# Attention, expert layer and soft mixture on one core: small steps and weight conversion spread over the rounds, reciprocals spread by DRAM transfers, chunk sums added on VectorE

## The chip, the core and the metric

The kernel runs on one core of one Trainium2 chip. The metric is the device time of one execution in microseconds (us), as the median of three runs. Engines are named as the profile names them: PE is TensorE (PEld its weight load), DVE is VectorE, ACT is ScalarE, POOL is GpSimd, and SP is SyncE, whose queue issues most of the transfers.

## The reference

```python
# attention: q, k, v are (4 batches, 12 heads, 448, 64)
q_n, k_n = rmsnorm(q, g_q), rmsnorm(k, g_k)
scores = q_n @ k_n.T / sqrt(64)
attn = exp(scores - max(scores)); attn = attn / (sum(attn) + 1e-9)
x = (attn @ v) as (1792, 768)
# expert layer: w_in (768, 2048), w_out (2048, 768)
y = relu(x @ w_in) ** 2 @ w_out
# soft mixture: phi (768, 32), w1 (8, 768, 1024), w2 (8, 1024, 768)
logits = y @ phi
d = softmax(logits, over tokens); slots = d.T @ y          # 32 rows
out_slots[e] = relu(slots[e] @ w1[e]) @ w2[e]
out = softmax(logits, over slots) @ out_slots
```

w_in and w_out arrive in 64-bit elements, so they are read as two 32-bit words each and turned into float32 by integer operations on the chip.

## The kernel before

Two heads of a batch make a pair; there are 24 pairs, six to a batch. A function `attention()` runs rounds t, and in each round the steps of a list, `ORDER` (lines 25 to 28). The table `blocks` gives every step an offset: in round t the loads are those of pair t+5, sums of squares and the root (a Newton iteration for 1/sqrt, on odd pairs and for two pairs at once) those of pair t+4, transposes t+3, row maxima t+2, scores (`s0` to `s3`), products with v (`v0` to `v3`) and the sums of exponentials t, and the reciprocals and the normalised output t-1. A pair's 448 rows are four chunks of 112; `nm` is a chunk's row maximum, `p_0` to `p_3` are its exponentials (112 x 896, both heads), `pss` the scores in PSUM.

The sums come from 16 instructions on PE with a matrix of ones (for each chunk four groups of rows). They are copied to `sm`, folded by small transfers into `rsh` (32 x 28), inverted there by VectorE (`rr`), sent back as two rows (`rs`), and spread over 128 partitions by PE with the 2 x 128 matrix `sel2`. VectorE multiplies the pair's output with that (`xf`), and splits it in two parts of reduced precision (`xh`).

Beside the attention the two weight matrices are converted in 32 units of 768 x 128, sixteen of each. A unit is fetched, gets three operations on VectorE (`wf`), two on ScalarE for the sign, one more on ScalarE, a product on POOL, and is stored to DRAM. A unit of w_out is also transposed on PE, copied (`wt`), and multiplied with phi (`wp`). The step `cvt` of a round calls `convert_stage`, which moves units on by a large stage: all three VectorE steps are issued at once. `CONVERT` says how many units may begin in each round.

Rounds before `PINNED` (6) keep their instructions in the order in which the program issues them (`InOrder`); in the later ones the tile scheduler may reorder. After the sixth pair of a batch a generator `moe_hidden(b)` begins, the hidden layer `ph` of that batch (16 columns of 18 products on PE, with the weights split as `whl` from the stored units); each step of `ORDER` gives it a credit of its cost times `PACE`. When the attention's buffers are released, the last batch's hidden layer and the experts follow, whose 1-MB weight pieces stream through a ring of buffers.

All helpers record through one line, so the profile names line 97 for nearly everything, and groups are told apart by their tiles.

Of the kernel before, what the change touches and what calls it, by code (L numbers as in the profile page):

```python
# [17 lines left out]
def raw(ap):  # L18
# [17 lines left out]
PINNED = 6  # L36
# [8 lines left out]
def tile_attention_moe_softmoe(  # L45
# [80 lines left out]
    sel2 = const.tile([2, 2, 64], F32, tag="sel2", name="sel2")  # L126
    nc.vector.tensor_copy(sel2, ident[0:2, 0:2, None].broadcast_to([2, 2, 64]))

# [94 lines left out]
    def root(t):  # L223
        if t % 2 == 0:
            return
        ss = live["ss"]
        ms = att.tile([CP, 32], F32, tag="ms", name=f"ms_{t}", bufs=2)
        y = att.tile([CP, 32], F32, tag="y", name=f"y_{t}", bufs=2)
        u = att.tile([CP, 32], F32, tag="u", name=f"u_{t}", bufs=2)
        dve.tensor_scalar(ms, ss, 1.0 / D, EPS, ALU.mult, ALU.add)  # L230
        dve.tensor_scalar(y.bitcast(I32), ms.bitcast(I32), 1, None, ALU.logical_shift_right)
        dve.tensor_scalar(y.bitcast(I32), y.bitcast(I32), -1, 0x5F3759DF, ALU.mult, ALU.add)
        for _ in range(3):
            dve.scalar_tensor_tensor(u, y, -0.5, y, ALU.mult, ALU.mult)
            dve.tensor_tensor(u, u, ms, ALU.mult)
            dve.scalar_tensor_tensor(y, u, 1.5, y, ALU.add, ALU.mult)
        for x in range(2):
            for i in range(2):
                a = 16 * x + 8 * i
                qk = live[t - 1 + x]["qk"][i]  # L240
                by = y[:, a : a + 8].rearrange("p (c h) -> p c h", h=2)[:, :, :, None]
                pool.tensor_tensor(qk, qk, by.broadcast_to([CP, NC, 2, D]), ALU.mult)
# [55 lines left out]
    def values(t, c):  # L298
# [3 lines left out]
        for j in range(2):  # L302
            for d in range(0, D, 32):
# [7 lines left out]
                )  # L311

    def sums(t):
        ps = mps()
        for x in range(2):
# [166 lines left out]
    def convert_next():  # L482
        convert_stage(True)
# [475 lines left out]
```

## Time and profile before

| what | us |
|---|---|
| median of 3 runs (lowest, highest) | 984.38 (982.26, 984.74) |
| profiled execution, device time | 984.84 |
| profiled execution, span from first to last instruction | 983.0 |
| PE busy | 832.9 (85%) |
| VectorE busy | 461.5 (47%) |
| ScalarE busy | 384.8 (39%) |
| POOL busy | 301.2 (31%) |

The mean granted clock of TensorE is 0.921 of full speed. A busy time is the sum of an engine's own instructions, so an engine at 85% may still be the limit in one stage and idle in another; the stages therefore stand apart in the rows below. The marks of the stages are events of the trace: 35.3 is the first instruction of PE, 68.5 the first scores of pair 0, 231.4 the end of the sums of pair 6, 440 that of pair 11, 760 that of pair 23.

### The profile page before, as it was taken

What the parts mean: (1) busy time and instruction counts of PE and PEld (TensorE: products, weight loads), DVE (VectorE), ACT (ScalarE), POOL (GpSimd) and SP (SyncE); (2) the same over time, 40 slices, a digit from 0 to 9 for tenths busy, and PEclk for the clock granted to TensorE, in tenths of its full rate; (3) what the DMA queues carried; (4) which work ended last, traced back from release to release, by engine and by line L of the source; (5) the groups of instructions that cost most, each with busy time, mean ns of one, the idle gap of its engine ahead of it and who ended that gap; (6) DMA issues with size and microseconds to landing.
All of it is one profiled execution on the core that took longest, in us unless ns stands there. A gap on an engine that the chain in (4) does not pass through costs nothing.

```text
span 983.0 us, 13480 instructions
## 1 busy us (share of the span) xinstructions
PE 832.9 (85%) x5298; PEld 490.5 (50%) x5298; DVE 461.5 (47%) x799; ACT 384.8 (39%) x598; POOL 301.2 (31%) x282
## 2 busy tenths in 40 slices
PE   0257777799888979989999998999999999889875
PEld 0133333345555646635566563556655588444433
DVE  4676575687832766455345346522312443411022
ACT  2435454566534555434334433433335243110011
POOL 4532323275734565320624323133222000000000
PEclk9999798759879989999999999999999899998795
DMA  8743333363253543202222220021121695699999
GB/s 270 211 123 95 121 110 110 102 194 98 97 157 95 180 154 112 77 26 65 63 62 64 78 77 26 28 74 42 49 59 34 236 367 184 253 370 363 347 348 294
DMA packets 113134, 142.87 MB, mean 145 GB/s; under 512 B 53296, under 2 KB 94768, under 8 KB 113072
## 3 DMA queue, kind: packets, MB, share of 16 engines
q1 hardware_dynamic: 100880, 84.61, 27.5%
q0 software_dynamic: 12192, 57.42, 18.1%
q8 instruction: 41, 0.67, 0.3%
q14 instruction: 21, 0.17, 0.1%
HBM read 123.57 MB, written 18.09 MB: 144 GB/s over the span
## 4 chain that ended last, share of the span: by engine, by line
PE 55%; DVE 12%; issue 8%; DMA 8%; POOL 7%; ACT 5%; SPq 4%; POOLq 0%; DVEq 0%; ACTq 0%
PE ph L97 18%; PE pm L97 16%; PE pss L97 6%; PE pv L97 6%; SPq L97 4%; PE pe L97 4%; DVE wf L97 4%; PE so_ps L97 2%; POOL whl L97 2%; PE pt L97 2%; DMA qk<-in_q_dram 2%; POOL wf L97 2%; DVE nm L97 2%; DMA wr<-wi_s 1%; DMA w<-in_moe_w_dram 1%
## 5 line engine op out<-in xcount | busy, mean ns | idle before, releaser
L97 PE MATMUL ph<-xh,whl 128*128 128x448 f32 x1152 | 281.0, 387 | 7.9 <-ACT gt L97 7.0
L97 PEld LDWEIGHTS ph<-xh,whl 128*128 128x128 f32 x1152 | 213.0, 194 | 68.7 <-issue 36.4
L97 DVE TENSOR_REDUCE nm<-pss 112x2 f32<-112x896 f32 x96 | 103.5, 1080 | 65.8 <-PE pss L97 65.6
L97 ACT ACTIVATE p<-pss 112x896 f32<-112x896 f32 x96 | 87.7, 915 | 89.3 <-PE pss L97 89.3
L97 POOL TENSOR_TENSOR whl<-wr,whl 128x768 fp32r<-128x768 f32 x45 | 84.5, 1877 | 123.3 <-ACT whl L97 116.6
L97 POOL TENSOR_TENSOR wf<-wf,w 128x768 f32<-128x768 f32 x32 | 64.5, 2018 | 141.9 <-ACT wf L97 116.5
L97 PE MATMUL pv<-p,vf 112*32 112x448 f32 x768 | 106.7, 595 | 0.3 <-ACT p L97 0.3
L97 ACT ACTIVATE gt<-ph 128x448 f32<-128x448 f32 x64 | 34.7, 542 | 122.8 <-PE ph L97 122.8
L97 ACT ACTIVATE w<-w 128x768 int32<-128x768 f32 (+2 forms) x68 | 58.6, 865 | 54.2 <-DVE wf L97 28.8
L97 POOL TENSOR_TENSOR gt<-gt 128x448 f32<-128x448 f32 x33 | 31.3, 949 | 152.6 <-ACT gt L97 146.0
L97 PE MATMUL pm<-ident,qk 112*128 112x112 f32 x192 | 31.7, 295 | 40.9 <-DMA vf<-in_v_dram 35.3
L97 PE MATMUL pss<-kh,qh 64*112 64x448 f32 x192 | 44.1, 453 | 25.8 <-DVE nm L97 16.8
L97 POOL TENSOR_TENSOR qk<-qk,y 112x512 f32<-112x512 f32 x48 | 49.5, 1054 | 32.9 <-DVE y L97 32.9
L97 PEld LDWEIGHTS pm<-ident,qk 112*128 112x128 f32 x192 | 22.9, 157 | 62.0 <-POOL qk L97 41.5
L97 PE MATMUL pm<-p,ones 112*32 112x448 f32 x384 | 50.5, 609 | 0.0
L97 DVE TENSOR_TENSOR ql<-pm,qh 128x448 fp32r<-128x448 f32 x24 | 15.0, 624 | 74.7 <-ACT qh L97 74.7
L97 PE MATMUL pss<-qh,kh 64*112 64x448 f32 x192 | 45.7, 468 | 4.3 <-ACT p L97 4.3
L97 DVE TENSOR_REDUCE ss<-sq 112x8 f32<-112x512 f32 x48 | 32.4, 676 | 30.5 <-ACT sq L97 30.3
L97 ACT CAST whl<-wr 128x768 fp32r<-128x768 f32 x50 | 41.3, 827 | 8.0 <-DMA wr<-wi_s 7.9
L97 ACT ACTIVATE sq<-qk 112x512 f32<-112x512 f32 x48 | 29.9, 625 | 32.5 <-DMA qk<-in_q_dram 26.4
L97 PEld LDWEIGHTS pss<-kh,qh 64*112 64x112 f32 x192 | 18.5, 187 | 46.9 <-DVE nm L97 25.8
L97 PE MATMUL pm<-ident,gt 128*112 128x128 f32 x256 | 39.1, 285 | 2.0 <-DVE lsb L97 1.6
(149 smaller groups left out, 1173.4 us busy)
## 6 DMA issues: line engine op xcount, KB each, us to landing
w<-in_moe_w_dram SPq DMA_DIRECT2D x48, 1024.0 KB
wr<-wi_s POOLq DMA_DIRECT2D x50, 384.0 KB, 3.4
w<-in_moe_w_in_dram POOLq DMA_DIRECT2D x16, 768.0 KB, 6.8
w<-in_moe_w_out_dram POOLq DMA_DIRECT2D x16, 768.0 KB, 5.7
wi_s<-wf POOLq DMA_DIRECT2D x16, 384.0 KB, 3.2
wo_s<-wf POOLq DMA_DIRECT2D x16, 384.0 KB, 2.9
wo<-wo_s SPq DMA_DIRECT2D x6, 1024.0 KB
qk<-in_q_dram SPq DMA_DIRECT2D x48, 112.0 KB
```

Of the source, the lines that this page charges most:

```text
L97: ins = f(*args, **kw)
```

## The change

There are five edits. The list `ORDER` is rewritten: loads, squares and roots run one pair further ahead, the transposes stand ahead of the last product with v, the output of a pair comes one round later and early in it, and seven rounds are held in written order. The root is cut in three steps. The conversion becomes a generator that does one small stage at each of four `cvt` slots of a held round, and three at a slot afterwards. The reciprocals go to a DRAM tile and are read back over 64 partitions each by two transfers (`rb`), and the product with `sel2` is gone. From pair 7 on VectorE adds exponentials of two chunks (`fold`), and PE sums half as many tiles.

```diff
 ORDER = (
-    "loadv load s0 mx0 cvt row sq0 s1 mx1 v0 cvt sq1 root recip "
-    "s2 mx2 v1 cvt s3 mx3 v2 out v3 sum trans0 trans1 cvt"
+    "loadv load s0 mx0 row sq0 cvt out s1 mx1 v0 sq1 cvt s2 mx2 v1 recip cvt root0 "
+    "s3 mx3 v2 cvt root1 trans0 trans1 v3 sum root2"
 ).split()
-LEAD = 5
-CONVERT = [1, 1, 1, 1, 1, 1, 2, 1, 2, 1, 2, 3, 3, 3, 3, 3, 3]
+LEAD = 6
+CONVERT = [1, 1, 1, 1, 1, 1, 1, 1, 1, 1, 1, 1, 1, 3, 3, 3, 3, 3, 3, 3]
-PINNED = 6
+PINNED = 7
...
+    def newton():
+        ms, y, u = live["root"]
+        dve.scalar_tensor_tensor(u, y, -0.5, y, ALU.mult, ALU.mult)
+        dve.tensor_tensor(u, u, ms, ALU.mult)
+        dve.scalar_tensor_tensor(y, u, 1.5, y, ALU.add, ALU.mult)
-    def root(t):
+    def root(t, part):
         if t % 2 == 0:
             return
...
+        if part == 0:
...
+        elif part == 1:
+            newton()
+            newton()
+        else:
+            newton()
+            for x in range(2):
...
+                    pool.tensor_tensor(qk, qk, by.broadcast_to([CP, NC, 2, D]), ALU.mult)
...
+        if c % 2 and t >= PINNED:
+            fold(t, c)
+    def fold(t, c):
+        p, p1 = live[t][f"p{c - 1}"], live[t][f"p{c}"]
+        dve.tensor_tensor(p1, p1, p, ALU.add)
     def sums(t):
         ps = mps()
-        for x in range(2):
+        folded = t >= PINNED
+        for x in (1,) if folded else (0, 1):
             for j in range(2):
                 for i in range(2):
                     g = 32 * (2 * j + i)
-                    mm(ps[g : g + 32, :S], ones, live[t][f"p{2 * x + i}"][:, j, :], x == 0, x == 1)
-        tt = att.tile([128, S], F32, tag="t", name=f"t_{t}", bufs=2)
+                    c = 2 * i + 1 if folded else 2 * x + i
+                    mm(ps[g : g + 32, :S], ones, live[t][f"p{c}"][:, j, :], folded or x == 0, x == 1)
+        tt = att.tile([128, S], F32, tag="t", name=f"t_{t}", bufs=3)
...
-        rs = att.tile([2, S], F32, tag="rs", name=f"rs_{t}", bufs=2)
+        rs = dram.tile([2, S], F32, tag="rs", name=f"rs_{t}", bufs=2)
         sp.dma_start(rs.rearrange("j (r e) -> j r e", r=16), rr)
-        live[t]["rs"] = rs
+        rb = att.tile([128, S], F32, tag="rb", name=f"rb_{t}", bufs=1)
+        for j in range(2):
+            sp.dma_start(rb[64 * j : 64 * j + 64, :], rs[j : j + 1, :].broadcast_to([64, S]))
+        live[t]["rb"] = rb
     def normalise(t):
-        tt, rs = live[t]["t"], live[t]["rs"]
-        ps = mps()
-        mm(ps[:, :S], sel2.rearrange("p j d -> p (j d)"), rs)
         x = xp.tile([128, S], F32, tag="xf", name=f"xf_{t}", bufs=6)
-        dve.tensor_tensor(x, tt, ps[:, :S], ALU.mult)
+        dve.tensor_tensor(x, live[t]["t"], live[t]["rb"], ALU.mult)
...
     blocks = {
-        "load": (5, 0, lambda t: load(t)),
+        "load": (6, 0, lambda t: load(t)),
-        "sq0": (4, 0, lambda t: square(t, 0)),
+        "sq0": (5, 0, lambda t: square(t, 0)),
...
-        "out": (-1, 0.8, lambda t: normalise(t)),
+        "out": (-2, 0, lambda t: normalise(t)),
     }
...
-        for t in range(-LEAD, NT + 1):
+        for t in range(-LEAD, NT + 2):
...
-                    convert_stage(todo > 0)
+                    convert_step(todo > 0, 1 if pin["on"] else 3)
...
         dve.tensor_scalar(fi, hi, 3, 0x40000000, ALU.logical_shift_left, ALU.bitwise_xor)
+        yield
         dve.scalar_tensor_tensor(fi, lo, 29, fi, ALU.logical_shift_right, ALU.bitwise_or)
+        yield
         dve.tensor_scalar(f, f, -3.0e38, 3.0e38, ALU.max, ALU.min)
...
         act.activation(lo, hi.bitcast(F32), AF.Copy, scale=0.500001 / SMALL)
+        yield
         act.activation(lo.bitcast(F32), lo, AF.Sign)
+        yield
         act.activation(f, f, AF.Abs)
         pool.tensor_tensor(f, f, lo.bitcast(F32), ALU.mult)
...
+    def convert_step(more, stages):
+        for unit in list(running):
+            for _ in range(stages):
+                if next(unit[2], 0) == 0:
+                    running.remove(unit)
+                    break
```

The first place is VectorE's queue in a held round with a root. Before, a conversion's three steps (`wf`) and the root (`ms`, `y`, `u`) stand together:

```order
L97 TENSOR_REDUCE nm_587<-pss_618 112x2
L97 TENSOR_SCALAR wf_631<-w_26_343 128x768
L97 SCALAR_TENSOR_TENSOR wf_631<-w_26_343,wf_631 128x768
L97 TENSOR_SCALAR wf_631<-wf_631 128x768
L97 TENSOR_REDUCE ss_443<-sq_1_637 112x8
L97 TENSOR_SCALAR ms_640<-ss_443 112x32
L97 TENSOR_SCALAR y_641<-ms_640 112x32
L97 TENSOR_SCALAR y_641<-y_641 112x32
L97 SCALAR_TENSOR_TENSOR u_642<-y_641 112x32
L97 TENSOR_TENSOR u_642<-u_642,ms_640 112x32
```

Now, in a round of that kind, row maxima (`nm`) stand between the steps of the conversion and between the parts of the root:

```order
L97 SCALAR_TENSOR_TENSOR wf_461<-w_11_247,wf_461 128x768
L97 TENSOR_REDUCE nm_445<-pss_500 112x2
L97 COPY wt_509<-pm_516 128x256
L97 TENSOR_SCALAR wf_461<-wf_461 128x768
L97 TENSOR_SCALAR ms_522<-ss_382 112x32
L97 TENSOR_SCALAR y_523<-ms_522 112x32
L97 TENSOR_SCALAR y_523<-y_523 112x32
L97 TENSOR_REDUCE nm_445<-pss_539 112x2
L97 COPY wp<-pm_547 128x32
L97 SCALAR_TENSOR_TENSOR u_524<-y_523 112x32
```

What moved is the row maximum: it no longer stands behind the whole root. The second place is PE's queue in a later round, with the hidden layer (`ph`) between the products of a pair. Before, the product with `sel` and eight rows for the sums (two instructions each) stand there:

```order
L97 MATMUL pv_1839<-p_2_1897,vf_1486 32x448 x4
L97 MATMUL pm_1985<-rs_1886,sel_85 128x448
L97 MATMUL ph_1994<-xh_1636,whl_1906 128x448 x9
L97 MATMUL pv_1839<-p_3_1963,vf_1486 32x448 x4
L97 MATMUL ph_1994<-xh_1636,whl_1906 128x448 x9
L97 MATMUL pm_2017<-p_0_1776,ones 32x448
L97 MATMUL pm_2017<-p_1_1815,ones 32x448
L97 MATMUL pm_2017<-p_0_1776,ones 32x448
L97 MATMUL pm_2017<-p_1_1815,ones 32x448
L97 MATMUL pm_2017<-p_2_1897,ones 32x448
L97 MATMUL pm_2017<-p_3_1963,ones 32x448
```

Now:

```order
L97 MATMUL pv_1743<-p_3_1853,vf_1456 32x448
L97 MATMUL pm_1890<-ident,qk_0_1117 128x112 x4
L97 MATMUL pm_1897<-ident,qk_1_1120 128x112 x4
L97 MATMUL pv_1743<-p_3_1853,vf_1456 32x448 x3
L97 MATMUL ph_1917<-xh_1680,whl_1820 128x448 x9
L97 MATMUL pm_1927<-p_1_1734,ones 32x448
L97 MATMUL ph_1917<-xh_1680,whl_1820 128x448
L97 MATMUL pm_1927<-p_3_1853,ones 32x448
L97 MATMUL pm_1927<-p_1_1734,ones 32x448
L97 MATMUL pm_1927<-p_3_1853,ones 32x448
```

The product with `sel` is gone, the sums read `p_1` and `p_3` alone, and the transposes of a later pair have come ahead of the last product with v. The third place is VectorE's queue between the reciprocals (`rr`) and the output (`xf`) that waits for them. Before, in a held round:

```order
L97 SCALAR_TENSOR_TENSOR rr_659<-rsh_549 32x28
L97 RECIPROCAL rr_659<-rr_659 32x28
L97 TENSOR_REDUCE nm_587<-pss_675 112x2
L97 TENSOR_REDUCE nm_587<-pss_699 112x2
L97 TENSOR_TENSOR xf_709<-t_545,pm_707 128x448
```

Now, where the two are nearest to each other, in a later round:

```order
L97 RECIPROCAL rr_3693<-rr_3693 32x28
L97 SCALAR_TENSOR_TENSOR y_3955<-u_3956,y_3955 112x32
L97 SCALAR_TENSOR_TENSOR u_3956<-y_3955 112x32
L97 TENSOR_TENSOR u_3956<-u_3956,ms_3954 112x32
L97 SCALAR_TENSOR_TENSOR y_3955<-u_3956,y_3955 112x32
L97 SCALAR_TENSOR_TENSOR u_3956<-y_3955 112x32
L97 TENSOR_TENSOR u_3956<-u_3956,ms_3954 112x32
L97 SCALAR_TENSOR_TENSOR y_3955<-u_3956,y_3955 112x32
L97 TENSOR_REDUCE nm_3565<-pss_3631 112x2
L97 TENSOR_TENSOR xf_3855<-t_3530,rb_3698 128x448
```

Here `xf` reads `rb`, which two transfers fill from DRAM, where it read a tile of PSUM that PE filled; seven small operations of a root and one row maximum stand between.

## Rows read from the trace of the kernel before

**Rows 1.** Busy time by stage: start:end, length, engines' busy time (instructions), clock, DMA share, GB/s
```profile
0.00:35.30 35.30, 0.00 (x0) 0.00 (x0) 16.30 (x43) 11.61 (x15) 16.17 (x25) 1.00 0.97 273
...
68.50:231.40 162.90, 129.97 (x810) 61.40 (x810) 112.40 (x192) 87.26 (x125) 61.66 (x56) 0.81 0.40 120
231.40:440.00 208.60, 183.16 (x1078) 114.88 (x1078) 119.40 (x180) 100.73 (x152) 104.15 (x95) 0.91 0.38 114
440.00:760.00 320.00, 310.73 (x1960) 183.26 (x1956) 128.35 (x229) 128.61 (x201) 99.52 (x90) 1.00 0.20 55
760.00:983.00 223.00, 193.59 (x1401) 121.01 (x1397) 62.18 (x120) 45.22 (x90) 2.74 (x2) 0.87 0.88 304
```

**Rows 2.** The same view by round, rounds 0 to 6 (order: PE, PEld, DVE, ACT, POOL)
```profile
68.50:87.70 19.20, 16.06 (x116) 8.53 (x115) 9.24 (x15) 9.79 (x14) 5.34 (x6) 0.91 0.39 124
87.70:114.90 27.20, 20.12 (x123) 9.12 (x122) 18.75 (x34) 13.44 (x19) 10.34 (x10) 0.81 0.38 118
114.90:133.00 18.10, 15.06 (x122) 7.88 (x121) 10.72 (x18) 9.63 (x14) 2.98 (x3) 1.00 0.33 99
133.00:160.60 27.60, 19.88 (x122) 8.67 (x121) 18.54 (x34) 13.39 (x19) 10.33 (x10) 0.81 0.38 114
160.60:180.25 19.65, 16.34 (x103) 6.64 (x103) 10.28 (x16) 9.16 (x13) 2.99 (x3) 0.83 0.32 94
180.25:209.70 29.45, 21.79 (x115) 10.44 (x114) 26.48 (x52) 17.87 (x26) 17.59 (x14) 0.66 0.45 126
209.70:231.40 21.70, 20.71 (x120) 10.11 (x120) 18.39 (x27) 13.98 (x22) 12.08 (x11) 0.75 0.55 162
```

**Rows 3.** Timeline of PE in round 1
```profile
100.48 0.46 PE L97 MATMUL pss<-kh,qh 64*112 64x448 f32 x2 [3.77 <-ACT p L97]
...
103.29 1.85 PE L97 MATMUL pm<-rs,sel 2*128 2x448 f32 x2 [0.73 <-DMA rs<-rr]
```

**Rows 4.** Chain of waits at 754 to 767: the sel product, the sums, the reciprocals' transfer
```profile
754.27 0.94 PE pm L97 x2
...
758.50 1.69 PE pm L97 x16
...
765.04 1.84 DMA rs<-rr
```

**Rows 5.** Timeline of VectorE in round 1
```profile
94.48 2.54 DVE L97 SCALAR_TENSOR_TENSOR wf<-w,wf 128x768 int32<-128x768 int32 x1
...
98.25 0.18 DVE L97 TENSOR_SCALAR ms<-ss 112x32 f32<-112x32 f32 x1
...
101.34 2.01 DVE L97 TENSOR_REDUCE nm<-pss 112x2 f32<-112x896 f32 x2
```

**Rows 6.** Timeline of PE before the first scores: start, length, instructions [idle before <-releaser]
```profile
47.45 1.54 PE L97 MATMUL pm<-ident,wf 128*128 128x128 f32 x6 [6.78 <-POOL wf L97]
...
66.54 2.01 PE L97 MATMUL pm<-ident,qk 112*128 112x112 f32 x8 [5.05 <-POOL qk L97]
```

**Rows 7.** DMA issues: count, KB each, us from issue to landing
```profile
wr<-wi_s POOLq DMA_DIRECT2D x50, 384.0 KB, 3.4
...
wo_s<-wf POOLq DMA_DIRECT2D x16, 384.0 KB, 2.9
```

**Rows 8.** VectorE's groups by form for three tiles: duration ns min/median/max, first and last start
```profile
L97 DVE TENSOR_TENSOR xf<-t,pm x24: 610/621/623, 105.2 to 768.0; 128x448 f32<-128x448 f32 x24
L97 DVE TENSOR_TENSOR xh<-xf,xh x24: 609/625/2081, 106.4 to 769.5; 128x448 fp32r<-128x448 f32 x24
...
L97 DVE TENSOR_TENSOR whl<-wi,whl x14: 948/952/960, 777.5 to 832.9; 128x768 fp32r<-128x768 f32 x14
```

**Rows 9.** PE's groups for a w_out unit: count | busy us, mean ns | idle before
```profile
L97 PE MATMUL pm<-phi_sb,wt 128*128 128x32 f32 x192 | 30.1, 304 | 8.2 <-ACT wt L97 5.9 <-DVE wt L97 2.2
...
L97 PE MATMUL pm<-ident,wf 128*128 128x128 f32 x96 | 17.2, 310 | 18.0 <-POOL wf L97 13.2 <-ACT sm L97 2.4 <-DVE kl L97 1.4
```

More of the change, by code (lines that the diff above doesn't have):

```diff
@@ L221, in square @@
         dve.tensor_reduce(live["ss"][:, a : a + 8], sq, AX.X, ALU.add)
-    def root(t):
+    def newton():
[4 more added lines that the diff above has]
+    def root(t, part):
         if t % 2 == 0:
             return
[L226 to L236, printed above, removed]
-        for x in range(2):
[L238 to L242, printed above, removed]
+        if part == 0:
+            ms, y, u = (att.tile([CP, 32], F32, tag=n, name=f"{n}_{t}", bufs=2) for n in ("ms", "y", "u"))
+            live["root"] = ms, y, u
+            dve.tensor_scalar(ms, live["ss"], 1.0 / D, EPS, ALU.mult, ALU.add)
+            dve.tensor_scalar(y.bitcast(I32), ms.bitcast(I32), 1, None, ALU.logical_shift_right)
+            dve.tensor_scalar(y.bitcast(I32), y.bitcast(I32), -1, 0x5F3759DF, ALU.mult, ALU.add)
+        elif part == 1:
[4 more added lines that the diff above has]
+            for x in range(2):
+                for i in range(2):
+                    a = 16 * x + 8 * i
+                    qk = live[t - 1 + x]["qk"][i]
+                    by = live["root"][1][:, a : a + 8].rearrange("p (c h) -> p c h", h=2)[:, :, :, None]
+                    pool.tensor_tensor(qk, qk, by.broadcast_to([CP, NC, 2, D]), ALU.mult)
     def trans(t, i):
@@ L350, in tile_attention_moe_softmoe @@
     blocks = {
[L351 removed]
+        "load": (6, 0, lambda t: load(t)),
         "loadv": (1, 0, lambda t: load_v(t)),
[L353 to L355 removed]
+        "sq0": (5, 0, lambda t: square(t, 0)),
+        "sq1": (5, 0, lambda t: square(t, 1)),
+        "root0": (5, 0, lambda t: root(t, 0)),
+        "root1": (5, 0, lambda t: root(t, 1)),
+        "root2": (5, 0, lambda t: root(t, 2)),
         "trans0": (3, 0.4, lambda t: trans(t, 0)),
@@ L419, in convert @@
         dve.tensor_scalar(fi, hi, 3, 0x40000000, ALU.logical_shift_left, ALU.bitwise_xor)
+        yield
         dve.scalar_tensor_tensor(fi, lo, 29, fi, ALU.logical_shift_right, ALU.bitwise_or)
+        yield
         dve.tensor_scalar(f, f, -3.0e38, 3.0e38, ALU.max, ALU.min)
[L422 to L425 removed]
         act.activation(lo, hi.bitcast(F32), AF.Copy, scale=0.500001 / SMALL)
+        yield
         act.activation(lo.bitcast(F32), lo, AF.Sign)
+        yield
         act.activation(f, f, AF.Abs)
         pool.tensor_tensor(f, f, lo.bitcast(F32), ALU.mult)
[L431 to L442 removed]
+        prefetch()
+        yield
+        yield
+        dst = wi_s if kind == "in" else wo_s
+        pool.dma_start(dst[fc], f.rearrange("p k f -> p (k f)"))
+        if kind == "out":
+            wt = wst.tile([128, KC, 128], F32, tag="wt", name=name("wt"), bufs=1)
+            pss = []
+            for a, z in ((0, 4), (4, KC)):
+                ps = mps()
+                for kc in range(a, z):
+                    pe.transpose(ps[:, (kc - a) * 128 : (kc - a + 1) * 128], f[:, kc, :], ident)
+                src = ps[:, : (z - a) * 128].rearrange("p (k f) -> p k f", f=128)
+                copy(ON_WT[1 + (a > 0)], wt[:, a:z, :], src)
+            yield
+            ps = mps()
+            for kc in range(KC):
+                mm(ps[:, :NS], wt[:, kc, :], phi_sb[:, kc, :], kc == 0, kc == KC - 1)
+            copy(ON_WT[0], wp[:, fc, :], ps[:, :NS])
     units = []
@@ L475, in convert_stage @@
                 fetched[key] = fetch64(*key)
-            w64 = fetched.pop(key)
-            signed.append((*key, w64, convert(*key, w64)))
-            prefetch()
-        if not (units or signed or stored):
+            gen = convert(*key, fetched.pop(key))
+            next(gen)
+            running.append((*key, gen))
+            if not state["h0"]:
+                prefetch()
+        if not (units or running):
             state["cv"] = False
     def convert_next():
-        convert_stage(True)
+        convert_step(True, 3)
     def ensure(kind, fc):
-        while any(u[:2] == (kind, fc) for u in units + signed + stored):
+        while any(u[:2] == (kind, fc) for u in units + running):
             convert_next()
```

36 lines of the change are left out of this document (2 added, 34 removed).

## The prediction, made before the changed kernel had run

> **What bounds the kernel now.** I read the busy times by stage first [rows 1], because the average over 983 us mixes stages with different limits. The reader is to see five of them. From the first score to the end of the seventh pair's sums (68.5 to 231.4) TensorE works 130 of 162.9 us at a granted clock of 0.81, and no other engine is above 113: nobody is full, so order and waits decide. From 231.4 to 440 it works 183 of 208.6, and from 440 to 760 it works 310.7 of 320: there every instruction taken from TensorE is time, and 9.3 us of idling is all that waits cost. From 760 on the DMA share is 0.88; that stage has no edit of this change but the end of the last pair. Before 68.5 TensorE has little to do and waits for operands.
>
> Then the stage that waits, round by round [rows 2]. A round with no root and one conversion lasts 18.1 to 19.65 us. A round with a root and two conversions lasts 27.2, 27.6 and 29.45. The difference, 8 to 10 us, comes every second round. TensorE's timeline in the first of the long rounds says where [rows 3]: 3.77 us for a tile of exponentials, then 0.73 for the reciprocals, and then a product at 1.85 for two instructions, twice the 0.94 that it costs late in the kernel [rows 4]. The granted clock of that round is 0.81, so part of it ran at the lower of the two levels, 1.2 instead of 2.4 GHz; it is 1.00 in the shortest round, which has no such gap. VectorE's timeline of the same place [rows 5] names the owner: from 94.48 a conversion step of 2.54 with the next step and a sum behind it, from 98.25 twelve small root operations and the reciprocal's two, and only at 101.34 two row maxima that the next scores want. Ahead of the stage TensorE waits in the same way twice, 6.78 for a converted tile that it is to transpose and 5.05 for the scaled q and k that the root feeds [rows 6].
>
> **The change part by part.**
>
> *Spread root and conversion, pinned rounds.* Work is not removed: the same three conversion steps and twelve root operations are issued, but at most one conversion step or six root operations stand between two row maxima. Seven rounds are now held in written order; by the end of the seventh thirteen units have been started instead of seventeen, so each round has one. A round then looks like the short rounds of before, plus half a root (fourteen operations from 98.25 to 101.34 are 0.22 each with their gaps, so twelve are 2.6 and half is 1.3 us). Of the short rounds I take the mean, 18.98 [rows 2], and leave the half root out because row maxima now stand between its parts and TensorE no longer waits for all of it at once. Bounds: 15.8 (what TensorE works in the short rounds, on average, so no wait left) and the present mean, 162.9/7 = 23.3. Sum: 7 x 18.98 = 132.9 in place of 162.9, so -30.0 (-52 to 0).
>
> *Start of the stage.* Loads run six pairs ahead and roots are a round earlier, so the 5.05 wait for scaled q and k should go, and the transposes of a converted tile stand at the round's end and no longer hold the queue for 6.78. But the loads share a DMA system that is at 0.97 until 35.3 [rows 1], and one more round of small work has to go through VectorE and POOL. Bounds: -11.8 (both waits gone) and +5.05 (the wait doubled, if the extra round of small work comes in series). I take -4, near the 5.05 of a root that is a round ahead; the other wait is for a unit's whole conversion, which nothing shortens.
>
> *Reciprocals by DRAM.* TensorE loses 24 products of two instructions, 0.94 each where the clock is 1.00 [rows 1, 4]; 17 of them lie between 231.4 and 760: 17 x 0.94 = 16.0, all of it in stages where TensorE is the limit. VectorE's xf keeps its size. Added are 48 issues on SyncE's queue and a round trip: rr into DRAM, and two transfers that spread it over 64 partitions each. The trace has no such transfer. A store into DRAM lands after 2.9 and a load from it after 3.4, of 384 KB [rows 7]; rr into SBUF takes 1.84 [rows 4]. So the trip is between 3.7 (two times 1.84) and 6.3, and I take 6.3, the rows with DRAM in them. It is hidden: xf now stands in the round after its reciprocals', and the order puts eight to twenty VectorE instructions between, where it put two row maxima before. Queued behind the two waiting transfers on SyncE are the rsh transfers of the next sums, which come most of a round later, and the loads, six pairs ahead. At the very end of the attention it shows: the last xf comes about 4.5 later, while the order leaves two columns of batch 2's hidden layer (36 products) behind the last sums, which fill it. I count +1 there (-1.84, the present transfer gone from the path, to +4.5).
>
> *Folds.* From pair 7 on VectorE adds p0 to p1 and p2 to p3 (112x896), and the sums take 8 instructions in place of 16. The sums cost 1.69 [rows 4], half is 0.845; 17 x 0.845 = 14.4 less on TensorE. A fold with both inputs in SBUF is sized from 448 columns at 0.625 and 768 at 0.952 [rows 8]: 1.02 ns a column, so 0.952 + 128 x 1.02 = 1.08 us, 34 of them = 37 us on VectorE, which is busy 248 of 528.6 there. What of it reaches TensorE lies between 0 and 37. The row for 440 to 760 is the nearest: with VectorE busy 128 us in pieces of such a size, TensorE idles 9.3. The whole stretch from 231.4 idles 34.7; 15% more VectorE work (37/248) makes 5. I take +5.
>
> *Later conversions.* Four units move behind 231.4. Only half of them are of the kind that TensorE transposes and multiplies: (17.2 + 30.1)/16 = 2.96 us each [rows 9], two of them +6. The fill's credit, 0.8 less a round, only moves hidden-layer products from one place to another in a stage where TensorE is full: 0.
>
> *Sum.* 68.5 - 4 = 64.5; 132.9; 528.6 - 16.0 - 14.4 + 6 + 5 = 509.2; 223 + 1 = 224. Together 930.6, and 1.84 that the profiled execution has outside its span (984.84 against 983.0): 932.4. That execution is 0.46 above the median of the three runs, so 932.0. I forecast 932.
>
> **The rivals.**
>
> *The held rounds stay long.* In the seven rounds a chain runs from scores through row maximum, transpose, a small transfer and exponentials back to TensorE; if this and not the lump sets the round, or the lower clock stays, the rounds keep their mean less the reciprocals' wait of 0.73 [rows 3], 22.5. For it: the seventh round of before, which has no root, still takes 21.7 at 0.75 [rows 2]. Against it: three rounds with one unit take under 20. 7 x 22.5 = 157.5 in place of 132.9: 957.
>
> *The folds are paid.* A fold stands between row maxima on VectorE's queue, and the row maxima release the scores' PSUM. If all 37 us come back as waits instead of 5: 964. Against it is the 310.7 of 320. The xh rows show a second price: the same instruction takes 0.625 in the middle and 2.08 at most, and xf, whose second input is in PSUM, never more than 0.623 [rows 8]. If each fold met that, 34 x (1.08 + 1.46) = 86 would be added in place of 5: 932 + 81 = 1013.
> The Trainium skill has the reason, on the page "SBUF — State Buffer", section "Who interferes with whom": a VectorE instruction with two SBUF inputs and a GpSimd instruction that reads SBUF lock each other out, for the whole instruction. By that rule the folds, and xf now too, since its reciprocals come from SBUF, can each stand behind a whole GpSimd product; the spread in the xh row agrees, and its middle, at the lowest value almost, says that the case is not met every time.
>
> *Slower: the round trip is late.* If xf reaches the head of VectorE's queue before its reciprocals have come, everything behind it, row maxima first, stands still. At the tightest place of the order seven root operations of some 0.22 and one row maximum of 1.0 [rows 5] lie between, 2.5 us, against a trip of 6.3: 3.8 short. If each of 24 pairs loses that on TensorE's path, 24 x 3.8 = 91: 932 + 91 = 1023. It decides from 52/24 = 2.2 us a pair. Against it: the usual distance in the order is half a round, 8 us or more, and VectorE is busy less than half of the time from 231.4 on [rows 1].
>
> *It does not do what it says.* If the small steps are spread in the order but the waits are ACT's and POOL's, who keep their work, only TensorE's saved products remain, with the clock as it is, and the folds take half back: about 975 to 990. The order speaks against it on VectorE; for POOL it says little.
>
> **How the numbers follow.** Forecast 0.62; long rounds 0.18; folds paid 0.09 (of it 0.01 with the second price); late round trip 0.06; no effect 0.05. The forecast's own range is 912 to 950: the start -6 to +9, the rounds -10 to +11, the folds -5 to +15, the last pair -3 to +4, not all at once. To leave no more than 2 in 10 out it takes in the rounds that stay long and most of the paid folds: 908 to 966. A difference under 0.3%, 3 us, cannot be told from none here. Faster by more than that: the first three cases less the second price, and 0.02 of the last, 0.62 + 0.18 + 0.08 + 0.02 = 0.90; within it the rest of the last, 0.03; slower 0.06 + 0.01 = 0.07.
>
> **What would show it.** Right: held rounds of 18 to 20 us each, with no odd-even pattern; TensorE's waits for exponentials under 1.5 us there and its granted clock above 0.9; no product of the reciprocals; sums of 8 instructions at about 0.85; xf starting without a wait for rb; the stretch from the seventh sums to the last near 510. Wrong: VectorE idling for rb, row maxima late behind folds of 2 us and more, held rounds above 21, or a stage after the last sums longer than 228.

## The result, and the profile after

The changed kernel takes 907.98 us (median of three runs, 905.28 to 915.75), against 984.38: the ratio is 0.9247 with a 95% interval of 0.9156 to 0.9337. Timed a second time, beside other kernels, it took 910.06 at the median of six (901.52 to 915.25), and the ratio, 0.9259 (0.9207 to 0.9312), leaves out the 915.25, which counts as a slow run; without it the median is 908.73. Its profiled execution is the slowest of the first three, 915.75 with a span of 914.0, so the stages below are read against 915.75, not against the median. From one run to the next this kernel moves by 1.5%, more than the 0.3% that I took as the bound; differences of 4 us between two variants are not settled by the runs here.

Busy time by stage, the stages cut at the same events as in [rows 1] (first scores, end of the seventh sums, end of the last sums); the columns are PE, PEld, DVE, ACT, POOL, the granted clock, the DMA share and GB/s:

```profile
0.00:60.34 60.34, 15.46 (x59) 9.92 (x59) 42.80 (x83) 24.54 (x35) 35.69 (x40) 1.00 0.78 225
60.34:179.26 118.92, 102.51 (x788) 49.38 (x788) 95.34 (x176) 76.04 (x112) 46.53 (x43) 0.95 0.56 154
179.26:682.45 503.19, 460.57 (x2816) 283.67 (x2816) 302.40 (x446) 232.07 (x352) 225.25 (x195) 0.95 0.32 95
682.45:914.00 231.55, 203.41 (x1454) 130.07 (x1454) 67.24 (x128) 50.88 (x101) 7.31 (x7) 0.89 0.86 298
```

| stage | before | forecast | after | after, second profile |
|---|---|---|---|---|
| start | 68.5 | 64.5 | 60.3 | 60.8 |
| held rounds | 162.9 | 132.9 | 118.9 | 122.4 |
| seventh to last sums | 528.6 | 509.2 | 503.2 | 495.2 |
| after the last sums | 223.0 | 224 | 231.6 | 231.2 |
| span | 983.0 | 930.6 | 914.0 | 909.6 |

The held rounds carry 44 of the 69 us of span. TensorE's idle time in them fell from 32.9 to 16.4 us, and its busy time from 130.0 to 102.5. The 27.5 us of busy time are not all clock. The reciprocals' products are 9.15 of them, and the two units of w_out that moved behind this stage are some 6, against some 4 for instructions of later pairs that moved in. The rest, some 16 us, is the same instructions in less time, at a granted clock of 0.95 in place of 0.81 (an estimate, each group's mean before and after times its count). The stage's instructions that read `rs`, then those that read exponentials before and after, 336 in both (here with TensorE's busy time alone):

```profile
68.50:231.40 162.90, 9.15 (x12) 0.81 0.40 120
...
68.50:231.40 162.90, 50.39 (x336) 0.81 0.40 120
...
60.34:179.26 118.92, 41.68 (x336) 0.95 0.56 154
```

By round, rounds 0 to 6, from one pair's first scores to the next pair's, the last one to the seventh sums (the same columns):

```profile
60.34:76.20 15.86, 14.92 (x116) 7.52 (x116) 14.06 (x30) 10.83 (x16) 7.08 (x8) 1.00 0.71 204
76.20:90.40 14.20, 11.77 (x103) 5.08 (x99) 11.03 (x14) 9.21 (x13) 6.58 (x7) 1.00 0.49 134
90.40:105.60 15.20, 14.46 (x123) 7.39 (x119) 12.47 (x30) 10.04 (x15) 4.76 (x4) 1.00 0.52 141
105.60:123.60 18.00, 15.78 (x121) 8.10 (x117) 12.49 (x18) 10.19 (x15) 6.59 (x7) 0.91 0.45 131
123.60:137.80 14.20, 12.98 (x106) 5.80 (x102) 11.95 (x28) 9.65 (x14) 4.46 (x4) 1.00 0.50 134
137.80:154.90 17.10, 14.25 (x122) 7.31 (x118) 12.67 (x18) 10.06 (x15) 6.60 (x7) 1.00 0.52 138
154.90:179.20 24.30, 18.29 (x124) 8.11 (x124) 20.68 (x38) 15.99 (x24) 10.41 (x9) 0.84 0.65 180
```

Against [rows 2] the long rounds with a root are gone (the root now falls in rounds 0, 2, 4 and 6), and five rounds of seven run at 1.00. The 24.30 of the last reaches to its sums; the next pair's scores begin at 169.12, only 14.2 us after its own. VectorE's groups for the three tiles of the change and of [rows 8], as duration min/median/max in ns:

```profile
L97 DVE TENSOR_TENSOR xf<-t,rb x24: 612/620/3142, 94.1 to 695.3; 128x448 f32<-128x448 f32 x24
...
L97 DVE TENSOR_TENSOR xh<-xf,xh x24: 549/616/1395, 97.1 to 698.0; 128x448 fp32r<-128x448 f32 x24
```
```profile
L97 DVE TENSOR_TENSOR p<-p,p x34: 1076/1092/3039, 195.4 to 679.9; 112x896 f32<-112x896 f32 x34
```

A fold takes 1.09 at the median, as sized, but up to 3.04; and xf, which never took more than 0.623 with its second input in PSUM, takes up to 3.14 now that both are in SBUF.

### The profile page after: what moved, and what is told of

It reads as the page before. It is cut to its first block, busy times and chain, and to the rows that moved or that the text cites. A ratio compares the mean times of both kernels' runs of the same rounds, so it can differ in the third digit from the quotient of the medians.

```text
span 914.0 us, 13256 instructions
## 1 busy us (share of the span) xinstructions
PE 782.0 (86%) x5114; PEld 473.0 (52%) x5114; DVE 507.8 (56%) x832; ACT 383.5 (42%) x598; POOL 314.8 (34%) x282
## 4 chain that ended last, share of the span: by engine, by line
PE 55%; DVE 14%; DMA 11%; issue 7%; POOL 6%; ACT 4%; SPq 1%; ACTq 0%; DVEq 0%; POOLq 0%
PE ph L97 20%; PE pm L97 12%; PE pss L97 7%; PE pv L97 6%; PE pe L97 4%; DVE wf L97 4%; POOL whl L97 3%; DMA wr<-wi_s 3%; DVE nm L97 3%; PE so_ps L97 2%; PE pt L97 2%; DMA qk<-in_q_dram 2%; DMA w<-in_moe_w_out_dram 2%; DMA w<-in_moe_w_dram 1%; POOL wf L97 1%
## 5 line engine op out<-in xcount | busy, mean ns | idle before, releaser
L97 POOL TENSOR_TENSOR whl<-wr,whl 128x768 fp32r<-128x768 f32 x45 | 93.2, 2070 | 104.0 <-ACT whl L97 93.9
L97 ACT ACTIVATE w<-w 128x768 int32<-128x768 f32 (+1 forms) x68 | 59.4, 875 | 40.7 <-DVE wf L97 32.1
L97 POOL TENSOR_TENSOR qk<-qk,y 112x512 f32<-112x512 f32 x48 | 52.8, 1125 | 44.1 <-DVE y L97 24.6
L97 PE MATMUL pm<-ident,qk 112*128 112x112 f32 x192 | 28.7, 293 | 43.9 <-POOL qk L97 32.9
L97 DVE TENSOR_TENSOR p<-p,p 112x896 f32<-112x896 f32 x34 | 44.3, 1304 | 23.4 <-PE pv L97 23.3
L97 PE MATMUL pss<-qh,kh 64*112 64x448 f32 x192 | 46.8, 460 | 10.1 <-ACT p L97 9.8
L97 PEld LDWEIGHTS pss<-qh,kh 64*112 64x112 f32 x192 | 17.6, 171 | 54.9 <-issue 28.3
L97 PEld LDWEIGHTS pm<-ident,gt 128*112 128x112 f32 x256 | 28.4, 137 | 32.6 <-issue 10.9
L97 DVE TENSOR_SCALAR wf<-w 128x768 int32<-128x768 int32 x32 | 40.2, 1257 | 8.0 <-DMA w<-in_moe_w_out_dram 4.4
```

The lines of the kernel that those rows point to most:

```text
L97: ins = f(*args, **kw)
```

## The experiments

All kernels are set beside the kernel before by their ratio, with its 95% interval; "the kernel again" is the changed kernel timed a second time, 0.9259 (0.9207 to 0.9312).

**The folds out.**

```diff
+FOLD = 99
...
-        if c % 2 and t >= PINNED:
+        if c % 2 and t >= FOLD:
...
-        folded = t >= PINNED
+        folded = t >= FOLD
```

Expected: 

> The changed kernel with the folds taken out: the sums take 16 instructions in every pair again, all else stays. My theory: 17 x 0.845 = 14 us come back on TensorE and 5 us of VectorE's crowding go, so about 9 us above the changed kernel (some 917), all of it between the seventh and the last sums. Rival, the folds are paid in full by waits behind them: 14 - 37 = 23 us below it (885). Rival, they cost nothing: 14 above (922). VectorE's busy time should fall by 44 us in each case.

Measured: 918.01 us, 0.9342 (0.9282 to 0.9402); VectorE's busy time fell from 507.8 to 458.7. The median is 8 to 10 above the changed kernel, as forecast, and excludes that the folds are paid in full. The intervals overlap a little, so the size is uncertain, and 14 (folds that cost nothing) is not excluded. The place was not found: the stage from the seventh to the last sums, where alone the folds act, takes 497.2, between the 503.2 and 495.2 of the changed kernel's two profiles.

```profile
184.40:681.60 497.20, 460.14 (x2950) 283.55 (x2949) 252.50 (x412) 231.99 (x350) 218.54 (x195) 0.97 0.33 96
```

**The folds from pair 12 on.** The same edit with 12 in place of 99.

Expected: 

> The folds begin at pair 12, when the conversions are done, instead of pair 7. My theory: where VectorE and POOL also convert, folds take about what they give (five pairs, 5 x 0.845 = 4 us given up, and some 5 to 8 of waits behind folds of 1.5 to 2.5 us gone), so 0 to 4 us below the changed kernel. Rival, folds are worth their 0.845 a pair everywhere: 4 us above. Rival, folds are worth nothing anywhere: the time of the kernel without them, 918.

Measured: 913.70, 0.9327 (0.9282 to 0.9371), 4 us above the kernel again by the medians and 7 by the ratios. That is nearer the rival's number than mine (folds give their 0.8 a pair also beside the conversions), but the intervals overlap, with those of the kernel without folds too, so none of the three is settled.

**The selecting product back.**

```diff
+    sel2 = const.tile([2, 2, 64], F32, tag="sel2", name="sel2")
+    nc.vector.tensor_copy(sel2, ident[0:2, 0:2, None].broadcast_to([2, 2, 64]))
...
-        rs = dram.tile([2, S], F32, tag="rs", name=f"rs_{t}", bufs=2)
+        rs = att.tile([2, S], F32, tag="rs", name=f"rs_{t}", bufs=2)
...
-        rb = att.tile([128, S], F32, tag="rb", name=f"rb_{t}", bufs=1)
-        for j in range(2):
-            sp.dma_start(rb[64 * j : 64 * j + 64, :], rs[j : j + 1, :].broadcast_to([64, S]))
-        live[t]["rb"] = rb
+        live[t]["rs"] = rs
...
-        dve.tensor_tensor(x, live[t]["t"], live[t]["rb"], ALU.mult)
+        ps = mps()
+        mm(ps[:, :S], sel2.rearrange("p j d -> p (j d)"), live[t]["rs"])
+        dve.tensor_tensor(x, live[t]["t"], ps[:, :S], ALU.mult)
```

Expected: 

> The changed kernel with the reciprocals sent back as two rows and spread by TensorE's product with the selecting matrix, at the place of the list where the output now stands. My theory: 24 products of 0.94 come back, 17 of them where TensorE is the limit, so 16 to 20 us above the changed kernel (some 926). Rival, the round trip by DRAM costs as much as it saves (VectorE waited 9.6 us for rb): 5 us or less above. Rival, the slower side: the kernel gets faster, below 903.

Measured: 921.85, 0.9374 (0.9328 to 0.9420), above the kernel again by 0.0115, 11 us, with intervals that don't touch. TensorE's busy time rose from 782.0 to 809.6. The sign and most of the size are as forecast, and so is the place: the stage from the seventh to the last sums takes 511.4 (503.2 and 495.2 in the changed kernel's profiles), the held rounds 119.2 (118.9 and 122.4). And xf, at the same place of the list but with its second input in PSUM again, takes 0.622 at most.

```profile
180.91:692.35 511.44, 484.75 (x2852) 291.25 (x2851) 293.26 (x448) 230.32 (x349) 220.89 (x195) 0.94 0.29 86
```
```profile
L97 DVE TENSOR_TENSOR xf<-t,pm x24: 549/608/622, 97.7 to 702.0; 128x448 f32<-128x448 f32 x24
```

**The spreading alone**: both edits together, so list, lead, small steps and the seventh held round without folds and without the DRAM way.

Expected: 

> The changed kernel without folds and with the selecting product back: the list, the lead, the small steps and the one more held round alone. If the parts add, 9 + 18 = 27 us above the changed kernel (some 935), so 49 of the 76 us belong to the spreading. Rival, both parts free TensorE in the same gaps and only one counts: 15 to 18 above (925). Held rounds should stay under 18.5 us in both.

Measured: 933.61, 0.9505 (0.9458 to 0.9551). The held rounds:

```profile
60.70:178.39 117.69, 105.61 (x794) 51.16 (x794) 93.60 (x177) 77.84 (x114) 43.35 (x42) 0.95 0.51 143
```

The parts add within the noise: 24 us above the kernel again, against 8 and 11 apart. 49 of the 76 us are the spreading's, and the held rounds are as short without the other two.

**Root and conversion in lumps**, with the new list, lead and one unit a round.

```diff
-        elif part == 1:
             newton()
             newton()
-        else:
             newton()
...
         dve.tensor_scalar(fi, hi, 3, 0x40000000, ALU.logical_shift_left, ALU.bitwise_xor)
-        yield
         dve.scalar_tensor_tensor(fi, lo, 29, fi, ALU.logical_shift_right, ALU.bitwise_or)
-        yield
         dve.tensor_scalar(f, f, -3.0e38, 3.0e38, ALU.max, ALU.min)
+        yield
         act.activation(lo, hi.bitcast(F32), AF.Copy, scale=0.500001 / SMALL)
-        yield
         act.activation(lo.bitcast(F32), lo, AF.Sign)
-        yield
...
         prefetch()
         yield
-        yield
```

Expected: 

> The changed kernel with list, lead and seven held rounds as they are, but the root in one piece and a unit's conversion in three large stages, its three VectorE steps together. My theory: the lumps make the long rounds, so the held rounds go from a mean of 17.0 back towards 22, with an odd-even pattern: 30 to 38 us above the changed kernel (some 942). Rival, the list's new order and the earlier root do it (scores no longer wait for what stands close ahead), not the small pieces: under 8 us above (916 at most), held rounds under 18.5.

Measured: 942.54, 0.9604 (0.9552 to 0.9656). The sum is what my theory said, and the place is not:

```profile
0.00:79.28 79.28, 18.85 (x79) 13.74 (x79) 43.49 (x87) 27.60 (x38) 41.14 (x46) 1.00 0.70 206
79.28:209.30 130.02, 103.06 (x779) 51.26 (x778) 101.93 (x181) 81.51 (x116) 47.80 (x42) 0.92 0.43 122
```

19 us are lost ahead of the first scores, 7 to 11 in the held rounds, whose mean is 18.6 and of which the first six take 14.2 to 19.0; the two longest of these have a root and the products of a w_out unit, but none is near the 27 of before. So the lump on VectorE does not by itself make before's rounds 23.3. What the start waits for stands in TensorE's timeline of this kernel:

```profile
44.58 1.54 PE L97 MATMUL pm<-ident,wf 128*128 128x128 f32 x6 [44.58 <-POOL wf L97]
...
48.95 1.73 PE L97 MATMUL pm<-ident,qk 112*128 112x112 f32 x8
...
72.92 1.54 PE L97 MATMUL pm<-ident,wf 128*128 128x128 f32 x6 [6.71 <-POOL wf L97]
```

TensorE's first instruction is now the transpose of a converted tile, and those of q and k, which begin at 32.85 in the changed kernel (its row stands with the transposes near, below), stand behind it until 48.95. That gave two theories to separate: VectorE's lump, and the distance on TensorE's queue between a unit's conversion and its transposes.

**Only VectorE's pieces in lumps**: root in one part, the three conversion steps together, and ScalarE, POOL and TensorE where they were. The root's edit is that of the lumps; the conversion's is this:

```diff
         dve.tensor_scalar(fi, hi, 3, 0x40000000, ALU.logical_shift_left, ALU.bitwise_xor)
-        yield
         dve.scalar_tensor_tensor(fi, lo, 29, fi, ALU.logical_shift_right, ALU.bitwise_or)
-        yield
         dve.tensor_scalar(f, f, -3.0e38, 3.0e38, ALU.max, ALU.min)
+        yield
+        yield
```

Expected: 

> The lumped kernel took 34 us more, but 19 of them ahead of the first scores, and its held rounds stayed at 18.6. Here VectorE's pieces alone are lumped (three steps of a conversion together, the root in one), while ScalarE's, POOL's and TensorE's parts of a unit stay at their present places. New theory: what counted is how far a unit's transposes stand behind its conversion on TensorE's queue, so 0 to 6 us above the changed kernel (908 to 914), first scores at 60 to 63. First theory, the forecast's (row maxima stand behind the lump): 25 us and more above, held rounds of 20 and more.

Measured: 934.75, 0.9521 (0.9469 to 0.9574); first scores at 65.6, held rounds 133.2. My new theory falls as the only cause: the lump costs some 25 us. TensorE's timeline shows longer waits for row maxima, 5.25 ahead of the first scores and 2.68 in the second round, where the changed kernel has 3.83 and 1.67:

```profile
63.26 0.71 PE L97 MATMUL pss<-kh,qh 64*112 64x448 f32 x2 [5.25 <-DVE nm L97]
...
91.67 0.46 PE L97 MATMUL pss<-kh,qh 64*112 64x448 f32 x2 [2.68 <-DVE nm L97]
...
106.76 0.67 PE L97 MATMUL ph<-xh,whl 128*128 128x448 f32 x2 [2.92 <-ACT xh L97]
```

They are not what recurs. From 30 to 200 us the waits for row maxima come to 14.3 us, and in the changed kernel to 12.3. New is the third row: four rounds from 106.76 on wait 2.8 to 2.9 each, 11.5 in all, for the pair's output, which the new list puts right behind the first conversion slot and so behind the lump. The lump is also longer than its instructions. Its middle step took 0.96 in the held rounds of the lumps, and here takes 2.5 in six rounds, each time beside GpSimd's product of another unit; the same holds for the 2.54 of [rows 5], where the same step of the unit before it took 0.96 (the lumps, then VectorE and GpSimd of this kernel):

```profile
98.90 0.96 DVE L97 SCALAR_TENSOR_TENSOR wf<-w,wf 128x768 int32<-128x768 int32 x1
...
102.36 2.50 DVE L97 SCALAR_TENSOR_TENSOR wf<-w,wf 128x768 int32<-128x768 int32 x1
...
101.96 2.09 POOL L97 TENSOR_TENSOR wf<-wf,w 128x768 f32<-128x768 f32 x1 [11.23 <-ACT wf L97]
```

**Small pieces, transposes near.**

```diff
         prefetch()
-        yield
-        yield
         dst = wi_s if kind == "in" else wo_s
```

Expected: 

> All small pieces stay as in the changed kernel; only the two empty stages between POOL's product of a unit and its store and transposes are taken out, so that TensorE's queue has the transposes at the slot of the product. New theory: TensorE stands behind POOL's tile again, in the start and in the held rounds with a w_out unit: first scores 5 to 15 us later, 10 to 25 us above the changed kernel (918 to 933), and waits for POOL's wf of 2 us and more on TensorE. Forecast's theory (only VectorE's lump counts): within 4 us of the changed kernel.

Measured: 931.68, 0.9514 (0.9461 to 0.9566); first scores at 65.3, held rounds 129.3. In the changed kernel the first transpose of a unit waits 0.55; here the first two wait as in [rows 6], and all five such waits from 30 to 200 us come to 20.3, most of the 22 to 25 us (the changed kernel, then this one, then its sum):

```profile
32.85 2.01 PE L97 MATMUL pm<-ident,qk 112*128 112x112 f32 x8 [32.85 <-POOL qk L97]
...
42.97 1.54 PE L97 MATMUL pm<-ident,wf 128*128 128x128 f32 x6 [0.55 <-POOL wf L97]
```
```profile
44.55 1.54 PE L97 MATMUL pm<-ident,wf 128*128 128x128 f32 x6 [5.49 <-POOL wf L97]
...
71.28 1.54 PE L97 MATMUL pm<-ident,wf 128*128 128x128 f32 x6 [3.22 <-POOL wf L97]
```
```profile
PE pm L97 <- POOL wf L97: 20.3, 5, 5.5
```

So both count, each for 22 to 26 us by itself, and together (the lumps) for 32 to 34. They do not add, and the lumps are not the sum of the two edits: there the lump does not meet GpSimd's product in the held rounds, its middle step takes 0.96 instead of 2.5, and the first six rounds take 16.6 on average where those of this section and the one before take 17.9 and 18.4 (15.8 and 16.3 in the changed kernel).

**The transposes of q and k last again.**

```diff
-    "s3 mx3 v2 cvt root1 trans0 trans1 v3 sum root2"
+    "s3 mx3 v2 cvt root1 v3 sum trans0 trans1 root2"
```

Expected: 

> The changed kernel with the two transpose steps back behind the last product with v and the sums, as in the list before. Theory: in a held round TensorE works on the transposes while ScalarE makes the last exponentials; without them ahead it waits 1 to 2 us a round, so held rounds of 18 to 19 and 8 to 15 us above the changed kernel (918 to 925). Rival: the place does not matter, within 4 us of 910.

Measured: 914.51, 0.9288 (0.9248 to 0.9328), 3 to 4 us above the kernel again, with intervals that overlap: the 8 to 15 us did not come, and whether the place costs anything in time is not settled. The held stage takes 117.0 in its profile, but it ends with the seventh sums, and these now stand ahead of the transposes. Up to the scores of the seventh pair, which have nearly the same instructions ahead of them in both (667 and 666), the six rounds are longer, 103.6 against 94.6 (97.7 in the second profile), so 1 to 1.5 us a round as the theory said, with one round of 24.7; the time does not show it.

```profile
60.45:164.07 103.62, 90.64 (x667) 46.27 (x667) 75.01 (x137) 60.46 (x88) 40.80 (x34) 0.90 0.48 134
...
60.34:154.90 94.56, 84.16 (x666) 41.20 (x666) 74.66 (x138) 59.99 (x88) 36.06 (x34) 0.98 0.53 147
```

**The kernel before with one unit a round.**

```diff
-CONVERT = [1, 1, 1, 1, 1, 1, 2, 1, 2, 1, 2, 3, 3, 3, 3, 3, 3]
+CONVERT = [1, 1, 1, 1, 1, 1, 1, 1, 1, 1, 1, 1, 3, 3, 3, 3, 3, 3, 3]
```

Expected: 

> The kernel before with one change: from pair 0 on one unit begins in each round up to the sixth pair's, not two or three, and three in each later one. Theory: the second unit makes the long odd rounds of before (two conversions and a root in a row ahead of the row maxima), so the held stage falls from 162.9 to about 140 to 148, some 5 to 8 us come back later, and the time is 965 to 975. Rival: root and list make them, within 4 us of the kernel before (982).

Measured: 983.82, 1.0004 (0.9969 to 1.0039): no change.

```profile
68.50:226.69 158.19, 127.63 (x775) 60.03 (x775) 103.14 (x180) 81.85 (x117) 52.02 (x51) 0.80 0.34 101
...
86.60:107.70 21.10, 15.94 (x100) 5.98 (x100) 13.20 (x28) 9.76 (x14) 6.96 (x7) 0.85 0.30 85
128.70:154.10 25.40, 22.12 (x125) 10.82 (x121) 13.80 (x30) 10.36 (x15) 6.96 (x7) 0.70 0.26 75
...
173.00:204.30 31.30, 21.48 (x124) 10.84 (x120) 29.34 (x55) 21.59 (x31) 15.24 (x13) 0.67 0.36 107
```

The stage loses 4.7 us and the clock stays at 0.80. The rounds with a root, 27.2, 27.6 and 29.45 before, take 21.1, 25.4 and 31.3 with one unit, the three others 18.1, 21.0 and 18.9. So the second unit is not what made the long rounds, but for some 2 us of each. Set beside the lumps (the same one unit a round, the same large pieces, held stage 130.0 at 0.92), what is left between the two kernels is the list's order, the loads and roots one round earlier, the seventh held round, smaller items of the change that no run takes out (one `sm` buffer in place of two, three of `t`, a unit's products with phi one slot behind its transposes) and the DRAM way, and the last of these is excluded by the spreading alone (117.7). Which item it is stays open.

**One more transfer in the reciprocals' way.**

```diff
         sp.dma_start(rs.rearrange("j (r e) -> j r e", r=16), rr)
+        rs2 = dram.tile([2, S], F32, tag="rs2", name=f"rs2_{t}", bufs=2)
+        sp.dma_start(rs2, rs)
...
-            sp.dma_start(rb[64 * j : 64 * j + 64, :], rs[j : j + 1, :].broadcast_to([64, S]))
+            sp.dma_start(rb[64 * j : 64 * j + 64, :], rs2[j : j + 1, :].broadcast_to([64, S]))
```

Expected: 

> The changed kernel with one more transfer in the reciprocals' way, DRAM to DRAM, 2 to 3 us more for each pair. Theory: the way is hidden but for the waits for rb already seen (9.6 us in 7 of 24 pairs), so 0 to 8 us above the changed kernel (910 to 918), the last pair's 2 to 3 among them. Rival (the slower side of the forecast): VectorE waits for it each time, 24 x 2.5 = 60 us above.

Measured: 900.81, 0.9137 (0.9102 to 0.9172): 7 to 9 us less than the changed kernel by the medians, which was not expected. VectorE does wait longer for rb, 12.9 us in all:

```profile
L97 DVE TENSOR_TENSOR xf<-t,rb 128x448 f32<-128x448 f32 x24 | 29.2, 1217 | 12.9 <-DMA rb<-rs 12.9
```

It rules the slower rival out. Why it is faster is not settled: in the two traces some 60 of VectorE's 832 instructions stand at another place, the first at 173 us and nearly all in the later rounds where the scheduler sets the order, so this need not be the longer way at all. Its later stage takes 485.7 where the changed kernel's takes 495 to 503.

**The small copies on ScalarE.** In the changed kernel TensorE's longest wait after the held rounds is for such a copy:

```profile
210.13 1.75 PE L97 MATMUL pm<-ident,qk 112*128 112x112 f32 x8 [8.77 <-DVE wt L97]
```
```diff
-ON_GN = [1, 0, 0, 1, 1, 1, 0, 1, 1, 0, 0, 0, 0, 0, 0, 1]
+ON_GN = [0, 0, 0, 0, 1, 1, 0, 1, 1, 0, 0, 0, 0, 0, 0, 1]
-ON_WT = [1, 0, 1]
+ON_WT = [0, 0, 0]
```

Expected: 

> The changed kernel with the small copies of a w_out unit (wt, wp) and of batch 0's columns (gn) all on ScalarE. Theory: after the held rounds TensorE waits for VectorE's copies that stand behind conversions and folds (wt 9 us, some wp and gn), and ScalarE is busy only 99 of 181 us there: 4 to 10 us below the changed kernel (900 to 906). Rival: ScalarE's exponentials stand behind the copies instead, and it is no faster, or 5 us slower.

Measured: 901.92, 0.9145 (0.9115 to 0.9174), below the changed kernel by 6 to 8 us by the medians, as expected. In its waits from the held rounds to the last sums no copy stands above 2.9 us:

```profile
PE pss L97 <- DVE nm L97: 10.1, 2, 6.0
...
PE pm L97 <- ACT wp L97: 2.9, 1, 2.9
...
PE pm L97 <- ACT wt L97: 1.6, 1, 1.6
```

The wait that the first profile had pointed to is gone. That it is worth the 8 us is likely, and not shown: waits for row maxima come to 10.1 in that stage, where they were 4.4.

**The changed kernel again.** Without an edit.

Expected: 

> The changed kernel itself, timed again, beside the other kernels of this job: its three runs so far went from 905 to 916, and the folds and the lumps are to be compared on one chip. Every theory expects 905 to 916, with a median near 908.

Measured: 910.06, as said. The copies on ScalarE (901.92) and the longer way of the reciprocals (900.81) are the two fastest kernels of all, and faster than both kernels of this case; no run has both edits in one kernel.

## Why the prediction was right, and where its steps were not

The forecast was 932 with a range from 908 to 966; the measured 907.98 lies on its lower edge, and 908.73 or 910.06 of the second time just inside, so that the range held is in part luck: it forecast 52 us and 76 came, and the narrower range of the forecast's own case, 912 to 950, did not hold them. Faster by more than 0.3% had 0.90. Of its own signs, two that were to say "wrong" came as well: VectorE idles for rb, and the stage after the last sums is longer than 228. By the stages, the forecast's span is 16.6 above the profiled one: 14.0 of it in the held rounds, 4.2 in the start, and -1.6 in the two later stages together.

*Start.* The step "the other wait is for a unit's whole conversion, which nothing shortens" was wrong. Nothing shortens the conversion, but its transposes now stand two empty stages later on TensorE's queue, so nothing waits for it: 0.55 in place of 6.78. With the stages taken out the first scores come 5 us later, with the lumps 19. So both waits went, not one. My -4 should have been nearer the sum of both, -11.8; it was -8.2, with other waits in their place (TensorE stands 4.93 for kh at 39.80 and 3.83 for a row maximum at 57.84).

*Held rounds.* The direction and the place were right, the owner only in part. I put the long rounds down to "a conversion step of 2.54", the second unit and the root standing ahead of two row maxima. Taking the second unit away from the kernel before changed nothing in the time, with large pieces under the new list the rounds still took 18.6, and the 2.54 is a step of 0.96 that met GpSimd's product. Small pieces on VectorE and the distance on TensorE's queue are worth 7 to 15 us of the stage. The list with the earlier root and what came with it is about 28 (158.2 against 130.0), but the lumps begin the stage 10.8 us later, so 17.4 are left up to the seventh sums (226.7 against 209.3). The size failed with it: I took the mean of before's short rounds, 18.98, as the floor of a round with less work, but these ran at 0.91, 1.00 and 0.83 and had gaps of their own; at 0.95 the mean is 17.0. Those rounds also still had the reciprocals' products, which the forecast counted behind 231.4 alone: 9.15 us of TensorE's work went here too. But the two kernels that keep the products have held rounds as short (117.7 and 119.2), so they do not explain the 14. Of the 44 us of the stage, some 16 are idle time, some 16 the clock, and the rest is work that is gone or moved.

*Reciprocals.* Forecast 16 saved in the later rounds; shown 11 in the whole kernel, with an uncertainty of some 7. The round trip was forecast at 6.3 and is 5.0 at the pair where VectorE runs into it, from the end of the reciprocal to xf:

```profile
667.93 0.32 DVE L97 RECIPROCAL rr<-rr 32x28 f32<-32x28 f32 x1
...
673.23 0.63 DVE L97 TENSOR_TENSOR xf<-t,rb 128x448 f32<-128x448 f32 x1 [0.28 <-DMA rb<-rs]
```

It is hidden for 17 pairs of 24. VectorE waits for rb at the other 7, 9.6 us in all and 4.1 at most, less than the 52 that the slower rival needed, and a longer way did not cost anything.

*Folds.* The sums of 8 instructions take 0.89 from their start to that of the next instruction where the 16 took 1.69 [rows 4], in the timeline of the changed kernel:

```profile
660.84 0.96 PE L97 MATMUL pm<-p,ones 112*32 112x448 f32 x8
661.73 0.46 PE L97 MATMUL pss<-qh,kh 64*112 64x448 f32 x2
```

The folds take 44.3 us on VectorE instead of 37, since some are late behind POOL. Net forecast 9; the medians say 8 to 10, with intervals that overlap and no place in the profile. The rival with the second price (86 us) did not come: the median fold is 1.09. That its mechanism exists is shown better than the forecast could: with its second input in PSUM xf takes 0.623 at most in [rows 8] and 0.622 at the same place of the new list, and with both in SBUF up to 3.14. This agrees with the Trainium skill, "SBUF — State Buffer", section "Who interferes with whom", where a second SBUF input is what brings VectorE and GpSimd into conflict. Either side pays. The longest xf stands beside three GpSimd products in a row, not one; and where xf falls into a GpSimd product and takes its usual 0.62, that product takes 2.62 instead of the 2.11 beside an xf that reads PSUM (xf and GpSimd in the changed kernel, at two places, then GpSimd with the selecting product back):

```profile
415.09 3.14 DVE L97 TENSOR_TENSOR xf<-t,rb 128x448 f32<-128x448 f32 x1 [1.06 <-DMA rb<-rs]
414.69 3.05 POOL L97 TENSOR_TENSOR qk<-qk,y 112x512 f32<-112x512 f32 x3
...
94.06 0.62 DVE L97 TENSOR_TENSOR xf<-t,rb 128x448 f32<-128x448 f32 x1
93.78 2.62 POOL L97 TENSOR_TENSOR wf<-wf,w 128x768 f32<-128x768 f32 x1 [10.71 <-ACT wf L97]
...
97.44 2.11 POOL L97 TENSOR_TENSOR wf<-wf,w 128x768 f32<-128x768 f32 x1 [11.87 <-ACT wf L97]
```

*After the last sums.* Forecast +1, measured +8.6, and the stage ahead of it came out 6.0 shorter than forecast. Work moved across the mark: 324 products of the hidden layer stand behind the last sums where 285 did, 71.2 us of TensorE in place of 62.0. I had counted the 36 that the order leaves there as filling a wait only (products that read `xh`, before and after):

```profile
760.14:983.00 222.86, 61.99 (x285) 0.87 0.88 304
...
682.45:914.00 231.55, 71.19 (x324) 0.89 0.86 298
```

With the seams left out, the two stages were forecast at 733.2 and took 734.8 (726.4 in the second profile).

## What to carry to other kernels

An instruction that waits for another engine's long chain should stand on its queue where the chain has long been done; here moving it two steps later was worth some 22 us. When a stage runs at a mean clock of 0.81, ask what it would take at 1.00 before taking its best rounds as the floor. And before a stall is put down to the piece that stands ahead of it, take that piece away in the old kernel: here the time did not move. A piece can also be long because of what runs beside it: the same step took 0.96 alone and 2.5 beside a GpSimd product.

## What was not expected of the hardware

The stores of converted units land later in the changed kernel: wo_s after 6.1 us at the median where it was 2.9 [rows 7], wi_s after 5.4 where it was 3.2. It goes with the two empty stages ahead of the store: with both taken out (the transposes near) they land after 4.6 and 3.2, with one out (the lumps) after 2.7 and 3.1. What delays them there, the runs do not say.
